# Channel attention and an ELU feed-forward layer on one core: Strassen's h product with another order of block and output products, one seeding copy a unit, high parts rounded by transfers, and other slots for side work

## The chip, the core and the metric

The kernel runs on one core of a Trainium2 chip. The engines named here are TensorE (PE; PEld is its weight load), VectorE (DVE), ScalarE (ACT), GpSimd (POOL) and SyncE (SP, which issues transfers). The metric is the device time of one execution in microseconds (us).

## The reference

q, k and v are fp32 arrays of 4 batches x 6080 tokens x 256 channels. Attention is over channels: q and k are normalised over the tokens, a 256 x 256 matrix per batch goes through a softmax, and v is multiplied with it. The result (24320 x 256) passes through a layer of width 2048 with an ELU and back to 256.

```python
qn = q / (norm(q, axis=1) + 1e-06); kn = k / (norm(k, axis=1) + 1e-06)
s = kn.transpose(0, 2, 1) @ qn / tau
a = softmax(s)                       # max taken off, sum + 1e-09
x = (v @ a).reshape(24320, 256)
h = x @ w_in                         # 256 x 2048
g = where(h > 0, h, exp(min(h, 0)) - 1)
out = g @ w_out                      # 2048 x 256
```

## The kernel before

For each batch the kernel forms W' = a @ w_in once (2048 columns, four quarters `fq` of 512), so that h = v @ W'. The tokens of a batch are 12 chunks `c` of 512 or 496; v comes in, and the output leaves, with channels first. Precision is kept by two-part products: a matrix is rounded to a TensorE format (its high part, `hi`), the rest is its low part (`lo`), and a product is hi·hi + hi·lo + lo·hi, three matmuls that add up in PSUM.

The first batch (to 598 us) is computed in another way and is not touched, apart from the preparation of the next chunk at its end. The other 36 chunks are 144 **units** (c, fq). In a unit the h product is a 2 x 2 block product by Strassen's scheme (Winograd's form) with seven block products of six matmuls each (`product`). Its left operands are blocks and sums of W' (A11, A22, A12, S1 to S4, in `s_tiles`, prepared per batch and quarter), its right operands blocks and sums of v (B11, B21, B22, T1 to T4, per chunk). With U = A11·B11 + S2·T2 the four results are h11 = A11·B11 + A12·B21, h22 = U + S1·T1 + S3·T3, h12 = U + S1·T1 + S4·B22 and h21 = U + S3·T3 + A22·T4. PSUM banks: `bank_a` for h11, two banks `b_0`, `b_1` in turn for U and what is added to it, `bank_e` for S3·T3 and A22·T4. ACT copies `bank_a` into the b bank to seed U, and twice copies the b bank to SBUF (L1468, L1476). VectorE adds `bank_e` to these copies (L1477 for h22, before A22·T4 is added to the bank; L1489 for h21).

Each of the four results goes through the ELU: a ReLU and an exponential on ACT (`relu_exp`, L1175 and L1176), a maximum on VectorE (`largest`, L1179). POOL rounds it (`hi_part`, L1182) and VectorE subtracts (`lo_part`, L1185); the parts stand in `g1` and `g2`, from a ring of three buffers. The output products of a unit (24 matmuls of 512 columns, L1116 to L1118) run in the unit behind it, in groups of one or two items between the block products (`multiply_out`).

Side work fills the engines beside this: v's T sums and block roundings for the next chunk (`t_sum`, `t_hi`, `t_lo`, `b_hi`, `b_lo`), and for the next batch the loads and roundings of q and k (`plan_rows`), the sums of squares, the gram matrix (matmuls put between output matmuls by `beside`), norms and softmax (`plan_soft`) and W' with its S sums (`plan_s`). A planner holds this work as tasks with an engine, a cost in us, a due time and the tasks that they depend on; at fixed places of a unit `spend(engine, budget, now)` writes out the tasks that are due and fit. `now` counts four to a unit (PERIOD). From the first unit on all five engines run in the order in which the code is written, so an instruction that waits holds up all behind it on its engine. Line numbers below are those of the kernel before, unless an order row of the changed kernel is shown.

## Time and profile before

| what | value |
|---|---|
| median of 2 runs | 2263.43 us (2261.64 to 2265.22) |
| profiled execution | 2265.94 us, span 2264.1 us |
| granted TensorE clock | 0.983 |
| busy: PE, PEld | 2156.0 us (95%), 1961.7 us (87%) |
| busy: VectorE, ACT, POOL | 1785.3 us (79%), 1543.3 us (68%), 850.7 us (38%) |
| transfers | 121.23 MB, DMA engines busy 16% by SP's queue |
| first unit's seeding copy | 598.4 us |

A row of the groups gives line, engine, operation, output and inputs, shapes and count, then the busy time and the mean of one in ns, then the idle time just before and what ended it. A row of the waits gives who waited for whom: us in total, times, longest. A row of the order in time gives start, duration, engine, line and, in brackets, idle time and what ended it. PE's busy time counts matmuls that overlap in its pipeline, so that the start of one to the start of the next is the better measure of PE's pace.

### The profile page before, as it was taken

Reading aid. Unit: us, or ns where it says so; the run is one execution under the profiler, and the core shown is the slowest. Engines: PE = TensorE matmul, PEld = TensorE weight load, DVE = VectorE, ACT = ScalarE, POOL = GpSimd, SP = SyncE. Lnnn points to the kernel's source line nnn. Section 1 sums busy time; section 2 is a strip of 40 time slices with the busy share of each in tenths; the row PEclk is TensorE's granted clock in tenths of the full one; section 3 lists DMA queues with packets and bytes.
Section 4 is the critical chain, followed back from the end, with each engine's and each line's share of the span. In section 5 each row is a group of like instructions: output and inputs, shape, how many; then the busy total and the mean of one; then the engine's idle time right before and its main releaser. Section 6 shows DMA issues by size and latency. Waiting matters only on the chain.

```text
span 2264.1 us, 34396 instructions
## 1 busy us (share of the span) xinstructions
PE 2156.0 (95%) x12834; PEld 1961.7 (87%) x12834; DVE 1785.3 (79%) x2514; ACT 1543.3 (68%) x2624; POOL 850.7 (38%) x1063
## 2 busy tenths in 40 slices
PE   9999999999899999899998999998999999999999
PEld 8888888899788888888888888887998888888898
DVE  7997777777788888786788888887778777777776
ACT  6877676667677777666566677775666666666665
POOL 0000000000355555535364555563456443444442
PEclk9999999999999999999999999999999999999999
DMA  9321222211211211100012222110100100100100
...
DMA packets 62567, 121.23 MB, mean 54 GB/s; under 512 B 6208, under 2 KB 16064, under 8 KB 62400
## 3 DMA queue, kind: packets, MB, share of 16 engines
...
q14 instruction: 67, 0.55, 0.1%
q10 hardware_dynamic: 144, 0.13, 0.0%
...
## 4 chain that ended last, share of the span: by engine, by line
PE 55%; DVE 17%; POOL 16%; issue 6%; ACT 5%; DMA 0%; POOLq 0%; ACTq 0%; DVEq 0%
POOL g L1182 7%; PE b L1093 5%; PE po L1116 5%; PE po L1118 5%; PE bank_e L1093 5%; PE po L1117 5%; DVE e_e L1179 4%; PE bank_a L1093 4%; PE ph L428 3%; PE ph L430 3%; PE ph L429 3%; DVE qk L1295 3%; PE po L472 3%; PE po L468 3%; PE po L470 3%
## 5 line engine op out<-in xcount | busy, mean ns | idle before, releaser
L1116 PE MATMUL po<-g,wo 128*128 128x512 f32 (+1 forms) x1158 | 447.6, 387 | 0.8 <-POOL g L1182 0.8
L1118 PE MATMUL po<-g,wo 128*128 128x512 f32 (+1 forms) x1158 | 445.2, 384 | 0.4 <-DVE g L1185 0.4
L1117 PE MATMUL po<-g,wo 128*128 128x512 f32 (+1 forms) x1158 | 445.3, 385 | 0.0
L1182 POOL CAST g<-e_e 128x512 fp32r<-128x512 f32 (+1 forms) x288 | 175.4, 609 | 619.5 <-DVE e_e L1179 605.2
L1093 PE MATMUL bank_e<-t,s 128*128 128x256 f32 (+1 forms) x1728 | 258.4, 287 | 98.7 <-DVE e_u L1477 91.7
L1093 PEld LDWEIGHTS bank_e<-t,s 128*128 128x128 f32 x1728 | 229.9, 198 | 129.2 <-DVE e_u L1477 116.4
L1185 DVE TENSOR_TENSOR g<-held,g 128x512 fp32r<-128x512 f32 (+1 forms) x288 | 283.7, 1021 | 73.3 <-POOL g L1182 73.3
L1182 POOL CAST g<-held 128x512 fp32r<-128x512 f32 (+1 forms) x288 | 228.4, 817 | 202.8 <-DVE held L1179 202.8
L1118 PEld LDWEIGHTS po<-g,wo 128*128 128x128 f32 x1158 | 223.7, 193 | 31.6 <-DVE g L1185 1.0
L1185 DVE TENSOR_TENSOR g<-e_e,g 128x512 fp32r<-128x512 f32 (+1 forms) x288 | 207.3, 720 | 52.7 <-POOL g L1182 42.7
L1093 PEld LDWEIGHTS b<-t,s 128*128 128x128 f32 x1728 | 233.4, 191 | 15.7 <-ACT held L1468 3.2
L1093 PE MATMUL b<-t,s 128*128 128x256 f32 (+1 forms) x1728 | 239.7, 275 | 3.0 <-ACT held L1468 2.1
L1175 ACT ACTIVATE e_e<-e_u 128x512 f32<-128x512 f32 (+1 forms) x144 | 90.3, 627 | 222.0 <-POOL g L1182 163.1
L1117 PEld LDWEIGHTS po<-g,wo 128*128 128x128 f32 x1158 | 225.2, 194 | 15.1
L1116 PEld LDWEIGHTS po<-g,wo 128*128 128x128 f32 x1158 | 224.9, 194 | 13.0 <-POOL g L1182 1.2
L1468 ACT COPY held<-b 128x512 f32<-128x512 f32 (+1 forms) x144 | 83.9, 583 | 169.0 <-PE b L1093 115.8
L1176 ACT ACTIVATE held<-held 128x512 f32<-128x512 f32 (+1 forms) x288 | 180.5, 627 | 9.1
L1176 ACT ACTIVATE e_e<-e_e 128x512 f32<-128x512 f32 (+1 forms) x288 | 180.5, 627 | 9.2
L1093 PE MATMUL bank_a<-s,s 128*128 128x256 f32 (+1 forms) x1296 | 186.2, 281 | 0.0
L1093 PEld LDWEIGHTS bank_a<-s,s 128*128 128x128 f32 x1296 | 178.1, 199 | 7.0
L169 POOL MEMSET raw<- 128x512 f32 x3 | 1.7, 578 | 457.0 <-DVE qk L115 457.0
L115 DVE TENSOR_TENSOR g<-e,g 128x512 fp32r<-128x512 f32 (+1 forms) x192 | 132.2, 688 | 48.9 <-ACT g L114 47.6
...
## 6 DMA issues: line engine op xcount, KB each, us to landing
raw<-in_q_dram SPq DMA_DIRECT2D x76, 256.0 KB, 2.7
raw<-in_k_dram SPq DMA_DIRECT2D x76, 256.0 KB, 3.0
v<-in_v_dram SPq DMA_DIRECT2D x32, 512.0 KB, 3.7
out_dram<-o SPq DMA_DIRECT2D x56, 256.0 KB, 2.0
...
wraw<-w_scr SPq DMA_DIRECT2D x12, 512.0 KB, 3.7
room<-in_q_dram SPq DMA_DIRECT2D x16, 256.0 KB, 5.2
```

Source lines behind the costliest of these rows:

```text
L115: nc.vector.tensor_sub(lo, src, hi.bitcast(F32))
L428: nc.tensor.matmul(ph[:, 0:n], w[:, kt, 0, fs], hi, start=(kt == 0), stop=False)
L1093: nc.tensor.matmul(bank[:, j, 0:hn], w[:, x, js], y, start=(begin and j == 0 and k == 0), stop=(j == 1 and k == 2), skip_group_check=True,)
L1116: yield nc.tensor.matmul(o, wo[:, f, 0, ds], hi, start=begin, stop=False)
L1117: yield nc.tensor.matmul(o, wo[:, f, 1, ds], hi, start=False, stop=False)
L1118: yield nc.tensor.matmul(o, wo[:, f, 0, ds], lo, start=False, stop=end)
L1175: nc.scalar.activation(e, h, AF.Relu, scale=-1.0)
L1176: nc.scalar.activation(e, e, AF.Exp, scale=-1.0)
L1179: nc.vector.scalar_tensor_tensor(e, e, -1.0, h, op0=ALU.add, op1=ALU.max)
L1182: nc.gpsimd.tensor_copy(g[:, :, 0, half, 0:hn], e)
L1185: nc.vector.tensor_sub(g[:, :, 1, half, 0:hn], e, g[:, :, 0, half, 0:hn].bitcast(F32))
L1468: nc.scalar.copy(e["u2"], vb)
```

## The change

- **Order and banks.** The block products keep their order (A11·B11, S3·T3, S2·T2, A12·B21, S1·T1, S4·B22, A22·T4); the output product between the last two now stands behind A22·T4. One bank `bank_b` takes the place of the two b banks. ACT seeds it with one copy of `bank_a` and copies S3·T3 to SBUF (`p7`). VectorE writes `bank_b` + `p7` back into `bank_e` behind S2·T2, and adds `bank_b` to `p7` behind S1·T1 (h22). A22·T4 then completes h21 in `bank_e`, S4·B22 completes h12 in `bank_b`; the ACT copies at L1468 and L1476 and the sum L1489 are gone.
- **High parts by transfers.** Transfers on POOL's queue that change the type take the place of POOL's and ACT's rounding instructions: all four blocks of g (`hi_part`), B11, B21 and B22 (from v in HBM), the w_in parts, the S parts of later batches, and the rows of q and k (read a second time from HBM). The squares of later batches are added to their sums by an accumulating transfer, 1024 elements at once, where VectorE or POOL added 512.
- **Low parts of g.** One subtraction of 1024 elements for g1 and one for g2, in the unit behind (`lo_parts`), where there were four of 512.
- **T.** The sums go from POOL to VectorE (three instructions for four), their rounding from POOL to ACT.
- **Slots.** The queues that several engines shared are gone; a task on POOL or PE may come no sooner than two steps of `now` behind what it needs from another engine, a subtraction behind a transfer no sooner than two steps. Tasks of the first two levels may pass one another. Norm and softmax steps are cut into single instructions, rows come 24 PERIODs to a batch for 23, a batch's plan starts a unit earlier, and budgets and places of `spend` are others.

VectorE in one late unit without side work, before (`e_` and `held` are the ELU blocks, `g1`, `g2` their two parts):

```order
L1179 SCALAR_TENSOR_TENSOR e_e11_5091<-e_e11_5091,bank_a_20589 128x2x248 [waits PE_49,Activation_49]
L1477 TENSOR_TENSOR e_u4_5090<-bank_e_20597,e_u4_5090 128x2x248 [waits Activation_49]
L1185 TENSOR_TENSOR g1_20639<-e_e11_5091,g1_20639 128x2x248 [waits Pool_49]
L1179 SCALAR_TENSOR_TENSOR e_e22_5092<-e_e22_5092,e_u4_5090 128x2x248 [waits DVE_49,Activation_49]
L1489 TENSOR_TENSOR held_5089<-bank_e_20597,held_5089 128x2x248 [waits PE_49]
L1185 TENSOR_TENSOR g2_20674<-e_e22_5092,g2_20674 128x2x248 [waits Pool_49]
```

The same engine at the start of such a unit now (`p7` holds S3·T3, then h22; DMASW are the completions of POOL's transfers):

```order
L1183 SCALAR_TENSOR_TENSOR held_5086<-held_5086,bank_e_20051 128x2x248 [waits PE_49,Activation_49]
L1189 TENSOR_TENSOR g1_20103<-held_5086,g1_20103 128x4x248 [waits DMASW2_49,DMASW0_49,DVE_49]
L1490 TENSOR_TENSOR bank_e_20144<-bank_b_5084,p7_5087 128x2x248 [waits PE_49,Activation_49]
L1189 TENSOR_TENSOR g2_20129<-held_5086,g2_20129 128x4x248 [waits DMASW3_49,DMASW1_49,DVE_49]
L1498 TENSOR_TENSOR p7_5087<-bank_b_5084,p7_5087 128x2x248 [waits DVE_49,PE_49]
```

The subtractions that waited for POOL now wait for transfers, and one stands ahead of each of the two sums. PE from S1·T1 to S4·B22 in a late unit, before (`b_0` is the bank of U, `po_` the output banks):

```order
L1093 MATMUL b_0_5085<-t_1_5094,s_2_4967 128x248 x5
L1116 MATMUL po_47_1_20742<-g1_20740,wo_83 128x496
L1117 MATMUL po_47_1_20742<-g1_20740,wo_83 128x496
L1118 MATMUL po_47_1_20742<-g1_20740,wo_83 128x496
L1116 MATMUL po_47_0_20726<-g1_20740,wo_83 128x496
L1117 MATMUL po_47_0_20726<-g1_20740,wo_83 128x496
L1118 MATMUL po_47_0_20726<-g1_20740,wo_83 128x496
L1093 MATMUL b_0_5085<-s_3_5093,s_2_4967 128x248 [waits Activation_49]
```

PE now, from S2·T2 over A12·B21 to S1·T1:

```order
L1102 MATMUL bank_b_5084<-t_1_5089,s_3_5088 128x248 x5
L1102 MATMUL bank_a_20334<-s_2_4966,s_3_5088 128x248 x6
L1125 MATMUL po_47_0_20189<-g1_20294,wo_83 128x496 [waits DMASW2_49,DMASW0_49]
L1126 MATMUL po_47_0_20189<-g1_20294,wo_83 128x496
L1127 MATMUL po_47_0_20189<-g1_20294,wo_83 128x496 [waits DVE_49]
L1102 MATMUL bank_b_5084<-t_1_5089,s_3_5088 128x248 [waits DVE_49]
```

The next product on the bank waited for ACT and now waits for VectorE, and the output product waits for two transfers and, at its low part, for VectorE. The diff, cut to its core:

```diff
--- before
+++ after
@@ -829,8 +829,12 @@
             lambda: sub(s4, a12, s2),
         )[k]()
 
-    def s_hi(b, fq, lo, hi, copy=nc.scalar.copy):
-        copy(s_tiles[fq][:, lo:hi, 0], x_of(b, fq, 1 + lo, 1 + hi))
+    def s_hi(b, fq, lo, hi, by_dma=False):
+        to, x = s_tiles[fq][:, lo:hi, 0], x_of(b, fq, 1 + lo, 1 + hi)
+        if by_dma:
+            nc.gpsimd.dma_start(to, x)
+        else:
+            nc.scalar.copy(to, x)
...
+    queues = {(e, level): [] for e in (ACT, DVE, POOL, PE, SP) for level in range(4)}
+    GAP = {ACT: 0, DVE: 0, POOL: 2, PE: 2, SP: 0}
 
     class Task:
         def __init__(self, fn, deps, when):
             self.fn, self.deps, self.when, self.done, self.cost = fn, deps, when, None, 0.0
 
-        def ready(self, now, gap):
-            return self.when <= now and all(d.done is not None and d.done + gap <= now for d in self.deps)
-
-    def task(engine, cost, fn, deps=(), when=0, level=1):
+        def ready(self, now):
+            if now < self.when:
+                return False
+            for d in self.deps:
+                if d.done is None:
...
     def spend(engine, budget, now):
-        order = [(engine, 0), (engine, 1), *((x, y) for x in SHARED.get(engine, ()) for y in range(2)), (engine, 2), (engine, 3)]
-        for key in order:
-            queue = queues[key]
-            while queue and queue[0].ready(now, 0):
-                t = queue[0]
-                cost = t.cost if key[0] == engine else t.cost[engine]
-                if cost > budget:
+        for level in range(4):
+            queue = queues[engine, level]
+            while True:
+                able = [t for t in (queue if level < 2 else queue[:1]) if t.ready(now)]
+                if not able or able[0].cost > budget:
                     break
-                queue.pop(0)
-                budget -= cost
-                if key[0] == engine:
-                    t.fn()
-                else:
-                    t.fn({ACT: nc.scalar.copy, DVE: nc.vector, POOL: nc.gpsimd.tensor_copy if key[0] == CAST else nc.gpsimd}[engine])
+                t = able[0]
+                queue.remove(t)
+                budget -= t.cost
+                t.fn()
...
@@ -1009,21 +1020,17 @@
         hn = half_of(c)
         if k == 0:
             state["tt", c] = work.tile([P, 4, HF], F32, tag="raw", bufs=5, name=f"tt_{c}")
-        v = vraw[c]
-        b11, b12 = (v[:, 0, x * hn : (x + 1) * hn] for x in range(2))
-        b21, b22 = (v[:, 1, x * hn : (x + 1) * hn] for x in range(2))
-        t1, t3, t2, t4 = (state["tt", c][:, y, 0:hn] for y in range(4))
-        sub, add = nc.gpsimd.tensor_sub, nc.gpsimd.tensor_add
+        v = vraw[c][:, :, 0 : 2 * hn].rearrange("p k (x t) -> p k x t", x=2)
+        tt = state["tt", c][:, :, 0:hn]
         (
-            lambda: sub(t1, b12, b11),
-            lambda: sub(t3, b22, b12),
-            lambda: add(t2, t3, b11),
-            lambda: sub(t4, b21, t2),
+            lambda: nc.vector.tensor_sub(tt[:, 0:2], v[:, :, 1], v[:, 0]),
+            lambda: nc.vector.tensor_add(tt[:, 2], tt[:, 1], v[:, 0, 0]),
+            lambda: nc.vector.tensor_sub(tt[:, 3], v[:, 1, 0], tt[:, 2]),
         )[k]()
 
     def t_hi(c, k):
         hn = half_of(c)
-        nc.gpsimd.tensor_copy(t_groups[c % 2][:, k : k + 2, 0, 0:hn], state["tt", c][:, k : k + 2, 0:hn])
+        nc.scalar.copy(t_groups[c % 2][:, k : k + 2, 0, 0:hn], state["tt", c][:, k : k + 2, 0:hn])
 
...
@@ -1043,8 +1050,10 @@
         return s_tiles[ring][:, SPARE], vraw[c][:, kt, x * hn : (x + 1) * hn], hn, name
 
     def b_hi(c, k):
-        to, src, hn, _ = block_of(c, k)
-        nc.gpsimd.tensor_copy(to[:, 0, 0:hn], src)
+        to, _, hn, _ = block_of(c, k)
+        _, kt, x = BLOCKS[k]
+        t0 = span(c)[1] + x * hn
+        nc.gpsimd.dma_start(to[:, 0, 0:hn], vT[kt * P : kt * P + P, t0 : t0 + hn])
 
     def b_lo(c, k):
...
@@ -1161,15 +1170,10 @@
         pos[NB - 1, dt] = last_po[dt]
     outs += [None] * 4
 
-    banks_b = [
-        ps.tile([P, 2, HF], F32, tag="w", bufs=WB, name="b_0"),
-        ps.tile([P, 2, HF], F32, tag="o", bufs=8 - KT - WB, name="b_1"),
-    ]
-    for bank in banks_b:
-        nc.tensor.matmul(bank, ones_r, wo[:, 0], start=True, stop=True)
-    held = work.tile([P, 4, 2, HF], F32, tag="qk", bufs=3, name="held")
-    e_tiles = {name: work.tile([P, 2, HF], F32, tag="e", bufs=3, name=f"e_{name}") for name in ("u4", "e11", "e22")}
-    e_tiles |= {name: held[:, x] for x, name in enumerate(("u2", "e12", "e21"))}
+    bank_b = ps.tile([P, 2, HF], F32, tag="o", bufs=8 - KT - WB, name="bank_b")
+    nc.tensor.matmul(bank_b, ones_r, wo[:, 0], start=True, stop=True)
+    held = work.tile([P, 2, 2, 2, HF], F32, tag="qk", bufs=3, name="held")
+    p7 = work.tile([P, 2, HF], F32, tag="e", bufs=3, name="p7")
 
     def relu_exp(e, h):
...
@@ -1179,10 +1183,14 @@
         nc.vector.scalar_tensor_tensor(e, e, -1.0, h, op0=ALU.add, op1=ALU.max)
 
     def hi_part(g, half, e, hn):
-        nc.gpsimd.tensor_copy(g[:, :, 0, half, 0:hn], e)
-
-    def lo_part(g, half, e, hn):
-        nc.vector.tensor_sub(g[:, :, 1, half, 0:hn], e, g[:, :, 0, half, 0:hn].bitcast(F32))
+        nc.gpsimd.dma_start(g[:, 0, :, half, 0:hn], e)
+
+    def lo_parts(g, x, hn):
+        nc.vector.tensor_sub(
+            g[:, 1].rearrange("p j r t -> p (j r) t")[:, :, 0:hn],
+            held[:, x].rearrange("p j r t -> p (j r) t")[:, :, 0:hn],
+            g[:, 0].rearrange("p j r t -> p (j r) t")[:, :, 0:hn].bitcast(F32),
+        )
 
 
...
@@ -1193,16 +1201,14 @@
         if c == NB:
             task(SP, 0, lambda: new_t_group(d), when=t, level=0)
         x = task(SP, 0, lambda: vraw.__setitem__(d, load_v(d)), when=t + PERIOD, level=0)
-        for k in range(4):
-            x = task(POOL, 0.65, lambda k=k: t_sum(d, k), [x], when=t + PERIOD, level=0)
-            if k % 2 == 1:
-                y = task(POOL, 0.65, lambda k=k: t_hi(d, k - 1), [x], when=t + PERIOD, level=0)
-                task(DVE, 0.685, lambda k=k: t_lo(d, k - 1), [y], when=t + PERIOD, level=0)
+        for k in range(3):
+            x = task(DVE, 0.415 if k else 0.685, lambda k=k: t_sum(d, k), [x], when=t + PERIOD, level=0)
+            if k != 1:
+                y = task(ACT, 0.61, lambda k=k: t_hi(d, k), [x], when=t + PERIOD, level=0)
+                task(DVE, 0.685, lambda k=k: t_lo(d, k), [y], when=t + PERIOD, level=0)
         for k, when in enumerate((2 * PERIOD, 3 * PERIOD, 3 * PERIOD + 1)):
-            y = task(POOL, 0.35, lambda k=k: b_hi(d, k), [x], when=t + when, level=0)
-            task(DVE, 0.415, lambda k=k: b_lo(d, k), [y], level=0)
-
-    BOTH = {ACT: 0.61, POOL: 0.65}
+            y = task(POOL, 0.55, lambda k=k: b_hi(d, k), when=t + when, level=0)
+            task(DVE, 0.415, lambda k=k: b_lo(d, k), [y, x], level=0, late=2)
 
     def plan_s(b, fq, t, norm_deps, early=False):
...
@@ -1447,64 +1468,71 @@
             plan_chunk(c)
         spend(SP, 1, now)
         assert (b, fq) in s_ready, (b, fq, u)
-        e = {name: t[:, :, 0:hn] for name, t in e_tiles.items()}
+        e11, e12, e21, e22 = (held[:, x, :, half, 0:hn] for x, half in ((0, 0), (0, 1), (1, 0), (1, 1)))
+        vp = p7[:, :, 0:hn]
         bank_a = ps.tile([P, 2, HF], F32, tag="w", bufs=WB, name="bank_a")
+        bank_e = ps.tile([P, 2, HF], F32, tag="w", bufs=WB, name="bank_e")
+        va, vb, ve = (bank[:, :, 0:hn] for bank in (bank_a, bank_b, bank_e))
+
         product(bank_a, c, fq, "A11", "B11", True)
-        bank_b = banks_b[u % 2]
-        va, vb = bank_a[:, :, 0:hn], bank_b[:, :, 0:hn]
+        if before is not None:
+            before[0]()
         nc.scalar.copy(vb, va)
-        bank_e = ps.tile([P, 2, HF], F32, tag="w", bufs=WB, name="bank_e")
-        ve = bank_e[:, :, 0:hn]
         product(bank_e, c, fq, "S3", "T3", True)
+        nc.scalar.copy(vp, ve)
         multiply_out(2, now)
+        spend(POOL, 3.9, now)
+        spend(ACT, 2.2, now)
+        spend(DVE, 2.8, now)
         if before is not None:
-            before()
-        spend(ACT, 1.9, now)
-        spend(POOL, 4.3, now)
-        spend(DVE, 2.5, now)
+            before[1]()
         product(bank_b, c, fq, "S2", "T2")
+        nc.vector.tensor_add(ve, vb, vp)
+        if before is not None:
+            before[2]()
         product(bank_a, c, fq, "A12", "B21")
+        relu_exp(e11, va)
+        spend(POOL, 0.6, now + 1)
         multiply_out(1, now)
-        nc.scalar.copy(e["u2"], vb)
         product(bank_b, c, fq, "S1", "T1")
-        relu_exp(e["e11"], va)
-        largest(e["e11"], va)
+        nc.vector.tensor_add(vp, vb, vp)
+        largest(e11, va)
         g1 = work.tile([P, 2, 2, 2, HF], F32R, tag="g", bufs=3, name="g1")
-        hi_part(g1, 0, e["e11"], hn)
-        spend(POOL, 1.3, now + 2)
-        multiply_out(2, now)
-        nc.scalar.copy(e["u4"], vb)
-        nc.vector.tensor_add(e["u4"], ve, e["u4"])
+        hi_part(g1, 0, e11, hn)
+        multiply_out(2, now + 2)
+        spend(ACT, 1.1, now + 2)
+        spend(DVE, 1.4, now + 2)
         product(bank_b, c, fq, "S4", "B22")
-        spend(ACT, 1.25, now + 2)
-        lo_part(g1, 0, e["e11"], hn)
-        spend(DVE, 1.0, now + 2)
-        multiply_out(1, now)
         product(bank_e, c, fq, "A22", "T4")
-        relu_exp(e["e22"], e["u4"])
-        largest(e["e22"], e["u4"])
-        multiply_out(2, now)
+        relu_exp(e22, vp)
+        largest(e22, vp)
+        multiply_out(1, now + 2)
         g2 = work.tile([P, 2, 2, 2, HF], F32R, tag="g", bufs=3, name="g2")
-        hi_part(g2, 1, e["e22"], hn)
-        nc.vector.tensor_add(e["u2"], ve, e["u2"])
-        relu_exp(e["e12"], vb)
-        relu_exp(e["e21"], e["u2"])
-        lo_part(g2, 1, e["e22"], hn)
-        largest(e["e12"], vb)
-        hi_part(g1, 1, e["e12"], hn)
-
-        def before(e=e, g1=g1, g2=g2, hn=hn):
-            largest(e["e21"], e["u2"])
-            hi_part(g2, 0, e["e21"], hn)
-            lo_part(g1, 1, e["e12"], hn)
-            lo_part(g2, 0, e["e21"], hn)
+        hi_part(g2, 1, e22, hn)
+        spend(DVE, 0.7, now + 2)
+        relu_exp(e12, vb)
+        relu_exp(e21, ve)
+        largest(e12, vb)
+        hi_part(g1, 1, e12, hn)
+        multiply_out(2, now + 2)
+
+        def finish(e21=e21, ve=ve, g2=g2, hn=hn):
+            largest(e21, ve)
+            hi_part(g2, 0, e21, hn)
+
+        before = (
+            finish,
+            lambda g1=g1, hn=hn: lo_parts(g1, 0, hn),
+            lambda g2=g2, hn=hn: lo_parts(g2, 1, hn),
+        )
```

155 lines of the change are left out of this document (88 added, 67 removed).

## The prediction

> **What bounds the kernel now.** I read the first part of the page, then the waits, then the once-a-unit copy by its line, then the order in time around one long unit. First the page and the copy that opens each unit (L1455, `bank_b` from `bank_a`).
>
> ```profile
> PE 2156.0 (95%) x12834; PEld 1961.7 (87%) x12834; DVE 1785.3 (79%) x2514; ACT 1543.3 (68%) x2624; POOL 850.7 (38%) x1063
> ...
> L1455 ACT COPY b<-bank_a x144: 557/578/590, 598.4 to 2243.4; 128x512 f32<-128x512 f32 x96, 128x496 f32<-128x496 f32 x48
> ...
> 1993.84 0.58 ACT L1455 COPY b<-bank_a 128x512 f32<-128x512 f32 x1
> 2003.71 0.58 ACT L1455 COPY b<-bank_a 128x512 f32<-128x512 f32 x1
> 2013.59 0.58 ACT L1455 COPY b<-bank_a 128x512 f32<-128x512 f32 x1
> 2027.15 0.57 ACT L1455 COPY b<-bank_a 128x512 f32<-128x512 f32 x1 [0.24 <-PE bank_a L1093]
> ...
> 2163.41 0.57 ACT L1455 COPY b<-bank_a 128x496 f32<-128x496 f32 x1
> 2173.13 0.56 ACT L1455 COPY b<-bank_a 128x496 f32<-128x496 f32 x1
> ...
> 633.99 0.58 ACT L1455 COPY b<-bank_a 128x512 f32<-128x512 f32 x1
> 645.15 0.58 ACT L1455 COPY b<-bank_a 128x512 f32<-128x512 f32 x1
> ```
>
> There are 144 units, from 598.4 to the end at 2264.1: 1665.7 us. An undisturbed unit takes 9.87 us with 512 tokens (2003.71 less 1993.84) and 9.72 with 496; one that also multiplies a group of rows into the gram matrix takes 11.16 (645.15 less 633.99). The unit that begins at 2013.59 takes 13.56 with the same matmuls as its neighbour. This is why:
>
> ```profile
> PEld bank_e L1093 <- DVE e_u L1477: 116.4, 63, 4.0
> DVE g L1185 <- POOL g L1182: 116.0, 331, 1.9
> ...
> PE bank_e L1093 <- DVE e_u L1477: 91.7, 48, 3.6
> ...
> DVE t L1031 <- POOL t L1026: 90.1, 70, 1.3
> ...
> 2018.42 1.21 DVE L1031 TENSOR_TENSOR t<-tt,t 128x512 fp32r<-128x512 f32 x1 [1.30 <-POOL t L1026]
> 2020.92 0.69 DVE L1031 TENSOR_TENSOR t<-tt,t 128x512 fp32r<-128x512 f32 x1 [1.29 <-POOL t L1026]
> 2021.53 0.68 DVE L1179 SCALAR_TENSOR_TENSOR e_e<-e_e,bank_a 128x512 f32<-128x512 f32 x1
> 2022.13 0.69 DVE L1477 TENSOR_TENSOR e_u<-bank_e,e_u 128x512 f32<-128x512 f32 x1
> ...
> 2020.10 0.38 PE L1117 MATMUL po<-g,wo 128*128 128x512 f32 x1
> 2020.32 0.38 PE L1118 MATMUL po<-g,wo 128*128 128x512 f32 x1
> 2022.87 0.94 PE L1093 MATMUL bank_e<-t,s 128*128 128x256 f32 x6 [2.18 <-DVE e_u L1477]
> ...
> 2024.35 0.63 PE L1116 MATMUL po<-g,wo 128*128 128x512 f32 x1
> 2024.77 0.63 PE L1117 MATMUL po<-g,wo 128*128 128x512 f32 x1
> ```
>
> VectorE stands twice behind POOL's rounding of the next chunk's T matrices, so L1477 is late; it must read `bank_e` before PE may add A22·T4 to it, and PE waits 2.18 us. After the wait, matmuls start 0.42 us apart (2024.77 less 2024.35) where they take 0.217 undisturbed (20.32 after 20.10), so a long wait is paid nearly twice. The floor of the unit stage is what PE needs without waits: 96×9.87 + 48×9.72 + 48 gram units (24 groups of rows in each of two batches) ×(11.16−9.87) + 96 matmuls for W' (two batches, four quarters, two halves, six each) ×0.217 = 948+467+62+21 = 1497. The profiled run (2265.94, span 2264.1, 1.8 around it; median of the shown runs 2263.43, 2.5 lower) loses 169 us to waits. With none it would be 598.4+1497+1.8 = **2097**.
>
> **The change part by part.** *The sums.* S3·T3 is copied to SBUF (`p7`); VectorE writes U+S3·T3 into `bank_e` right after S2·T2, three block products ahead of A22·T4, which then finds its bank ready. L1477's wait goes as a place: 92 us as PE shows it, up to the whole 169 with the slow restarts. What is late next is VectorE's two sums, each read by the next product on the single `bank_b`. As the rows of the section on the change show, `bank_b` was released for the next product by ACT and is now by VectorE, and the output product ahead of S1·T1 waits for two transfers and for VectorE. So VectorE's queue decides, and there each of the two sums (L1490, L1498) stands behind a low-part subtraction (L1189) that waits for transfers of the unit before. Queued behind that wait on VectorE are the sum, the maxima and all side work; PE waits for the sum with its next product, and ACT for the second sum with e22. That closes a loop, once round per unit: sum into `bank_e`, low parts of g2, sum into `p7`, ReLU and exp of e22, ReLU and exp of e12, its maximum, the transfer of its high part (L from the maximum's end to landing), low parts of g1, and again the sum. Prices:
>
> ```profile
> L1489 DVE TENSOR_TENSOR held<-bank_e,held 128x512 f32<-128x512 f32 (+1 forms) x144 | 97.7, 679 | 1.5 <-PE bank_e L1093 1.4
> ...
> L182 DVE TENSOR_TENSOR acc<-acc,sq x38: 1214/1225/1226, 10.5 to 502.0; 128x1024 f32<-128x1024 f32 x38
> ...
> L1175 ACT ACTIVATE held<-held 128x512 f32<-128x512 f32 (+1 forms) x144 | 90.5, 628 | 50.8 <-DVE held L1489 47.5 <-POOL g L1182 3.4
> ...
> L1175 ACT ACTIVATE held<-b 128x512 f32<-128x512 f32 (+1 forms) x144 | 83.0, 576 | 0.2 <-PE b L1093 0.2
> ...
> L1176 ACT ACTIVATE held<-held 128x512 f32<-128x512 f32 (+1 forms) x288 | 180.5, 627 | 9.1
> ...
> L1179 DVE SCALAR_TENSOR_TENSOR held<-held,b 128x512 f32<-128x512 f32 (+1 forms) x144 | 97.3, 676 | 0.0
> ...
> raw<-in_q_dram SPq DMA_DIRECT2D x76, 256.0 KB, 2.7
> raw<-in_k_dram SPq DMA_DIRECT2D x76, 256.0 KB, 3.0
> v<-in_v_dram SPq DMA_DIRECT2D x32, 512.0 KB, 3.7
> out_dram<-o SPq DMA_DIRECT2D x56, 256.0 KB, 2.0
> ...
> room<-in_q_dram SPq DMA_DIRECT2D x16, 256.0 KB, 5.2
> ```
>
> 0.68 + 1.22 + 0.68 + 0.63 + 0.63 + 0.58 + 0.63 + 0.68 + 1.22 = 6.95, with some 0.15 for handovers (my estimate) 7.1 + L. No transfer from SBUF to SBUF, none that rounds and none from POOL's queue is in this trace, so L is bounded by others of 256 KB: 2.0 (the store) below, 3.7 (twice the bytes) above, 5.2 where many are queued. I take 3.0, the second of two loads issued together, since it lands in SBUF as this one does and e22's transfer goes out just ahead of e12's. The loop is then 10.1, and the 96 units without gram, whose PE needs 9.81 on average (9.87 and 9.72), lose 0.29 each: 28 us. At L = 2.0 they lose nothing, at 3.7 they lose 96×0.99 = 95. Gram units (11.16) have 1.06 to spare, so for them the loop is hidden by PE up to L = 4.06.
>
> The Trainium skill (DMA: Bandwidth & Descriptors, "Anatomy of one DMA — SWDGE (gpsimd) path") gives such transfers 2.0 us plus the bytes at 436 GB/s, 2.6 us here: by it the loop would be 9.7 and the 28 us none.
>
> *Casts leave POOL and ACT.* The 576 roundings of g leave POOL, and with them the time that they and VectorE's subtractions took from each other: the same subtraction of 512 elements takes 0.72 us in one place and 1.02 in the other, and the same rounding 0.61 and 0.82.
>
> ```profile
> L1182 POOL CAST g<-held 128x512 fp32r<-128x512 f32 (+1 forms) x288 | 228.4, 817 | 202.8 <-DVE held L1179 202.8
> ...
> L1182 POOL CAST g<-e_e 128x512 fp32r<-128x512 f32 (+1 forms) x288 | 175.4, 609 | 619.5 <-DVE e_e L1179 605.2 <-PE bank_e L1093 9.4 <-PE bank_a L1093 2.5
> ...
> L1185 DVE TENSOR_TENSOR g<-held,g 128x512 fp32r<-128x512 f32 (+1 forms) x288 | 283.7, 1021 | 73.3 <-POOL g L1182 73.3
> ...
> L1185 DVE TENSOR_TENSOR g<-e_e,g 128x512 fp32r<-128x512 f32 (+1 forms) x288 | 207.3, 720 | 52.7 <-POOL g L1182 42.7
> ...
> L1278 POOL TENSOR_TENSOR acc<-acc,sq 128x512 f32<-128x512 f32 x71 | 113.7, 1619 | 0.1
> ...
> 2060.22 0.41 SPq L397 DMA_DIRECT2D v<-in_v_dram  x1
> ```
>
> VectorE's four subtractions, 2×1.02+2×0.72 = 3.48 us a unit, become two of 1.22: 1.0 us less, off the loop but cover for its side work. ACT, 68% busy, loses a copy (0.58) in each unit. POOL gains 848 transfers: 4.75 in a unit without gram (four of g, and three blocks of B in every four units), 7.75 with (two loads of rounded rows and one accumulation more). At 0.4 (SP's issue) to 1.62 (POOL's longest instruction) each, that is 1.9 to 7.7 of 9.81 us, and 3.1 to 12.6 of 11.16. I take the low end, for the issue is work of the same sort as SP's, and price it at nothing; the high end is the third rival. SP's own queue keeps its loads and stores.
>
> *Side work.* T sums go to VectorE ahead of g1's low parts: 0.68+2×0.42 = 1.5 us, beneath the transfer's cover there (L less the 1.3 of e21's ELU), 1.7: nothing; uncovered, 36×1.5 = 54. T's low parts stand ahead of e22's maximum while ACT still works on e22 for 1.26 us, 0.68 of it taken by e11's maximum: 72×0.1 = 7 not covered. Norm, softmax and S stages fill the first slot's budget of 2.8 against that 1.7 in some 16 units (a batch's norm and softmax cost about 9 us by the code's own costs, so four units, twice; and eight S sets): 16×1.1 = 18, between 0 and 16×2.8 = 45. Gram units move some 1 MB more from POOL's queue beside the loop; if that makes L longer by the 2.2 us between 3.0 and 5.2, 1.06 of it is spare and 48×1.1 = 55 is lost, otherwise 0; I take 10.
>
> Sum on the profiled run: 2097+28+7+18+10 = 2160; on the median 2158. Predicted **2160**.
>
> **Rivals.** *The wait comes back as a wait for the landing* (L about 3.8, or transfers whose descriptors wait for a VectorE instruction, 0.68 to 1.22): 96×(7.1+3.8−9.81) = 105, and with the 35 of side work 2097+105+35 = 2237, no change. For it: `DVE g<-POOL g` shows VectorE waiting 331 times already for a rounding of 0.61 to 0.82 us. Against: the 2.0 row. The Trainium skill (SBUF — State Buffer, "Who interferes with whom") says descriptor writing is locked out by VectorE's two-port modes, and that tensor_tensor has none; by it this would not happen here. 0.16.
>
> *It does not do what it says:* T's rounding now makes VectorE wait for ACT as it did for POOL; one wait of 2.2 us in each of the 36 chunks stays, though at another product: 36×2.2 = 79, 2097+79+28+35 = 2239. Against: ACT is 68% busy and the subtraction is placed a slot later. 0.06.
>
> *Slower: POOL's queue.* If one transfer holds it 1.62 us, 1.2 more than SP's issue, and e12's stands behind what is left of e22's, 0.6, L is 3.0+1.2+0.6 = 4.8: 96×2.09 = 200, gram units 48×1.4 = 67, 2097+267+35 = 2399. It is slower than before by 2% from L about 4.4 (96×1.7+48×0.35 = 180 on top of 2132). For it: the POOL rows here run from 0.61 to 1.62 us, none as short as SP's issue. Against: nothing shows its issue. 0.21.
>
> **How the numbers follow.** Forecast 0.57, the others 0.16, 0.06, 0.21. Two per cent (2218, 2309) is about what a measurement of this kernel can tell from no change: faster 0.57, same 0.22, slower 0.21. The range starts at the floor, 2100, and ends at L = 4.6 (2340), inside the slow case; some 0.15 lies outside.
>
> **What would show it.** The copy that opens a unit should come every 9.9 to 10.2 us in the late units, with no 13 us units; `bank_e` waiting for VectorE gone; PE's remaining waits on `bank_b` for L1490 and L1498; VectorE idle before L1189 for a transfer; L near 3.0; L1189 at 1.22. Wrong if L is over 4, or POOL is busy over 80%.

## The result, and the profile after

The changed kernel takes **2333.3 us** (median of two runs, 2332.99 to 2333.62), against 2263.43 before: a ratio of 1.031 (95% interval 1.026 to 1.035). It is slower by 3 per cent, where 2160 was forecast. The profiled execution took 2332.99, its span is 2331.2. In the late units, which multiply no rows, the forecast holds in sum; most of the time is lost in the stages that do.

The copy that opens a unit is L1480 now. Its rows in the order in time of the changed kernel, at units 4, 28, 100 and 143, counted from 0 (start, us, engine, line), then the same four of the kernel before without the first, which the prediction shows:

```profile
647.49 0.57 ACT L1480 COPY bank_b<-bank_a 128x512 f32<-128x512 f32 x1
...
976.85 0.57 ACT L1480 COPY bank_b<-bank_a 128x512 f32<-128x512 f32 x1
...
1872.61 0.57 ACT L1480 COPY bank_b<-bank_a 128x512 f32<-128x512 f32 x1 [0.88 <-PE bank_a L1102]
...
2308.08 0.56 ACT L1480 COPY bank_b<-bank_a 128x496 f32<-128x496 f32 x1 [0.87 <-PE bank_a L1102]
```

```profile
939.70 0.58 ACT L1455 COPY b<-bank_a 128x512 f32<-128x512 f32 x1
...
1789.01 0.58 ACT L1455 COPY b<-bank_a 128x512 f32<-128x512 f32 x1
...
2243.43 0.57 ACT L1455 COPY b<-bank_a 128x496 f32<-128x496 f32 x1
```

The 43 units from 100 to 143 took 454.4 us and take 435.5, 19 less. The 24 units from 4 to 28, most of them gram units, took 294.6 and take 329.4, 35 more; units 52 to 76, the second batch's, took 294.4 and take 316.1. Rows are now multiplied up to units 32 and 81, where they ended in units 27 and 75, and the units 28 to 48 and 76 to 96 together take 21 us more.

The page of the changed kernel (busy time of the engines; VectorE's low parts of g; then transfers with their count, size and median us from issue to landing), and behind it its waits (engine, tile and line, what it waited for: us in total, times, longest):

```profile
PE 2200.9 (94%) x12833; PEld 1967.5 (84%) x12833; DVE 1599.7 (69%) x2322; ACT 1419.1 (61%) x2380; POOL 633.4 (27%) x909
...
L1189 DVE TENSOR_TENSOR g<-held,g 128x1024 fp32r<-128x1024 f32 (+1 forms) x288 | 351.4, 1220 | 242.4 <-DMA g<-held 216.2
...
g<-held POOLq DMA_DIRECT2D x384, 256.0 KB, 2.5
...
acc<-sq POOLq DMA_DIRECT2D x46, 512.0 KB, 6.6
...
qk<-in_q_dram POOLq DMA_DIRECT2D x46, 256.0 KB, 6.6
```

```profile
DVE g L1189 <- DMA g<-held: 216.2, 112, 6.2
ACT sq L1287 <- DMA acc<-sq: 212.2, 29, 10.1
...
PE po L1125 <- DMA g<-held: 69.9, 33, 4.6
...
DVE t L1038 <- ACT t L1033: 59.8, 35, 2.3
...
PE bank_e L1102 <- DVE held L1183: 3.7, 10, 0.8
```

PE's 91.7 us of waiting for VectorE on `bank_e` are down to 3.7. In their place stand two waits for landings. VectorE waits 216 us for g, and ACT waits 212 us, in 29 places, for the accumulating transfer (L1290) to release the one buffer `sq` for the next group's square (L1287). The accumulate's median landing is 6.6 us after its issue, its 512 KB being twice the bytes of a transfer of g, which lands after 2.5.

One gram unit of the changed kernel in order of time, 15.25 us long. It is the first unit of its chunk; most such gram units take 15 to 17 us, most of the others 11 to 13:

```profile
1474.29 0.68 DVE L1183 SCALAR_TENSOR_TENSOR held<-held,bank_b 128x512 f32<-128x512 f32 x1
1474.33 0.72 POOL L1186 DMA_DIRECT2D g<-held  x1 [1.11 <-issue]
1474.43 0.38 SPq L397 DMA_DIRECT2D v<-in_v_dram  x1
...
1475.05 0.57 ACT L1480 COPY bank_b<-bank_a 128x512 f32<-128x512 f32 x1
1475.27 1.45 POOL L1186 DMA_DIRECT2D g<-held  x2 [0.21 <-issue]
...
1476.72 0.95 POOL L1290 DMA_DIRECT2D acc<-sq  x1
1477.30 0.92 POOL L1306 DMA_DIRECT2D qk<-in_q_dram  x1
...
1481.00 1.23 DVE L1189 TENSOR_TENSOR g<-held,g 128x1024 fp32r<-128x1024 f32 x1 [4.96 <-DMA g<-held]
...
1484.67 1.06 ACT L1287 ACTIVATE sq<-raw 128x1024 f32<-128x1024 f32 x1 [8.54 <-DMA acc<-sq]
1485.63 0.58 ACT L1179 ACTIVATE held<-bank_a 128x512 f32<-128x512 f32 x1
...
1490.30 0.57 ACT L1480 COPY bank_b<-bank_a 128x512 f32<-128x512 f32 x1
```

The transfer of e12's high part goes out at 1475.27 and has landed by 1481.00, after 5.7 us. Two transfers were issued within the microsecond ahead of it, e22's (1474.33) and SP's load of the next chunk's v (1474.43, 512 KB); e21's, the accumulate and the rows' transfers go out right behind it. So the delay of this one transfer can't be put down to those behind it alone. From the end of e12's maximum (1474.97) to the landing, the prediction's L is 6.0. The square has been ACT's next instruction since 1476.1 and stands there 8.54 us, until the accumulate issued at 1476.72 has landed. The unit's ReLU of e11 (1485.63) is queued behind it, though PE had completed its bank at 1477.65. These are two separate delays in one unit, and the experiments are there to price them apart.

How busy the DMA engines were in such stretches is read from the view of windows (window, its length, busy time of PE, PEld, DVE, ACT and POOL with counts, granted clock, the DMA engines' busy share, GB/s), for this gram unit, a calm one, units 4 to 28, and units 100 to 143:

```profile
1475.30:1481.00 5.70, 2.35 (x18) 2.10 (x17) 0.74 (x2) 0.83 (x2) 3.42 (x5) 1.00 1.12 290
...
2003.70:2006.30 2.60, 2.60 (x20) 2.44 (x19) 2.14 (x4) 1.56 (x4) 1.43 (x3) 1.00 0.85 224
...
647.50:976.80 329.30, 288.88 (x1729) 256.20 (x1728) 192.95 (x276) 169.31 (x282) 114.73 (x168) 0.94 0.75 190
1872.60:2308.10 435.50, 430.93 (x2841) 395.25 (x2839) 303.95 (x425) 276.43 (x473) 139.12 (x202) 1.00 0.52 136
```

```profile
645.15:939.70 294.55, 274.62 (x1763) 250.11 (x1762) 253.80 (x325) 207.94 (x364) 164.27 (x185) 0.99 0.18 58
```

The last row is units 4 to 28 of the kernel before: its DMA engines were busy 0.18 of the time, where they are 0.75 now. In the gram unit above they had hardly any free time while e12's transfer was under way (the share adds up the records of the packets, which can overlap, so it can pass 1). The same rows show a part of the loss that lies behind the waits: over units 4 to 28 the granted clock is 0.94, where it was 0.99, and PE is busy 289 us with 1729 matmuls, where the last kernel below needs 264 for 1730 at 1.00. So some 25 us of these units are matmuls that took longer, as the prediction had seen them do behind a wait.

### The profile page after: what moved, and what is told of

Read it like the earlier page. It is cut to its first block, busy times and chain, and to the rows that moved or that the text cites. A ratio compares the mean times of both kernels' runs of the same rounds, so it can differ in the third digit from the quotient of the medians.

```text
span 2331.2 us, 35484 instructions
## 1 busy us (share of the span) xinstructions
PE 2200.9 (94%) x12833; PEld 1967.5 (84%) x12833; DVE 1599.7 (69%) x2322; ACT 1419.1 (61%) x2380; POOL 633.4 (27%) x909
## 5 line engine op out<-in xcount | busy, mean ns | idle before, releaser
L1186 POOL DMA_DIRECT2D g<-held x576 | 409.8, 712 | 1061.1 <-issue 390.0
L1189 DVE TENSOR_TENSOR g<-held,g 128x1024 fp32r<-128x1024 f32 (+1 forms) x288 | 351.4, 1220 | 242.4 <-DMA g<-held 216.2
L1180 ACT ACTIVATE held<-held 128x512 f32<-128x512 f32 (+1 forms) x576 | 360.6, 626 | 18.3
L1102 PEld LDWEIGHTS bank_b<-t,s 128*128 128x128 f32 x1728 | 238.6, 201 | 48.2 <-DVE bank_e L1490 33.6
L1102 PE MATMUL bank_b<-t,s 128*128 128x256 f32 (+1 forms) x1728 | 263.4, 291 | 11.1 <-ACT bank_b L1480 3.2
L1179 ACT ACTIVATE held<-bank_a 128x512 f32<-128x512 f32 (+1 forms) x144 | 84.8, 589 | 241.9 <-PE bank_a L1102 103.2
L1287 ACT ACTIVATE sq<-raw 128x1024 f32<-128x1024 f32 x46 | 48.8, 1060 | 218.0 <-DMA acc<-sq 212.2
L114 ACT CAST g<-e 128x512 fp32r<-128x512 f32 (+1 forms) x192 | 116.7, 608 | 69.6 <-DVE e L445 37.6
L1183 DVE SCALAR_TENSOR_TENSOR held<-held,bank_a 128x512 f32<-128x512 f32 (+1 forms) x144 | 97.1, 674 | 85.7 <-ACT held L1180 85.7
L1480 ACT COPY bank_b<-bank_a 128x512 f32<-128x512 f32 (+1 forms) x144 | 81.6, 566 | 111.4 <-PE bank_a L1102 89.2
L1179 ACT ACTIVATE held<-p 128x512 f32<-128x512 f32 (+1 forms) x144 | 89.7, 623 | 91.3 <-DVE p L1498 91.3
```

What stands on the lines that cost most here:

```text
L114: nc.scalar.copy(hi, src)
L1102: nc.tensor.matmul(bank[:, j, 0:hn], w[:, x, js], y, start=(begin and j == 0 and k == 0), stop=(j == 1 and k == 2), skip_group_check=True,)
L1179: nc.scalar.activation(e, h, AF.Relu, scale=-1.0)
L1180: nc.scalar.activation(e, e, AF.Exp, scale=-1.0)
L1183: nc.vector.scalar_tensor_tensor(e, e, -1.0, h, op0=ALU.add, op1=ALU.max)
L1186: nc.gpsimd.dma_start(g[:, 0, :, half, 0:hn], e)
```

## The experiments

Two theories stood against each other. **A**: the square that waits for the accumulate stands in ACT's queue in front of the unit's ReLU and exp. **B**: the extra bytes (accumulate and rows, 1 MB a group of rows) delay the transfers of g that VectorE waits for. Edits are cut to their core, and line numbers shift by a few in the edited kernels. Each run was timed beside the kernel before, and the ratio to that (95% interval) stands in brackets.

### Each part undone by itself

The squares added on VectorE:

```
-    nc.gpsimd.dma_start(acc, sq, accum_op=ALU.add)      # task on POOL, level 2
+    nc.vector.tensor_add(acc[:, y], acc[:, y], sq[:, y]) # two tasks on VectorE, level 0
```

> The sums of the squares go back from the accumulating transfer (512 KB, landed after 6.6 us) to two additions of 512 elements on VectorE (0.69 us each); all else as in the changed kernel (2333). Theory A, the next square stands in ACT's queue ahead of the unit's ReLU and exp until the accumulate has landed in front of its one buffer (212 us of ACT's idle time): that wait goes, long gram units fall from 18.5 to about 13, time 2180 to 2230. Theory B, g's transfers land late because some 1 MB more per group passes through POOL's transfer queue: half the extra bytes go, so about half of the 173 us above the forecast, time 2240 to 2280, and VectorE's wait for g (216 us) falls to about half.

Measured: 2257.9 (0.997, 0.996 to 0.999). 75 us come back, not the 100 to 150 of theory A; the time, and VectorE's wait for g at half of 216, are what theory B had forecast. The waits of this kernel show another reason, a new wait, which a later run tests:

```profile
DVE g L1189 <- DMA g<-held: 106.5, 74, 4.0
...
DVE acc L1291 <- ACT sq L1287: 84.8, 29, 6.0
```

My additions may be placed in the slot in which the square itself was placed. VectorE reaches them before ACT reaches the square, and stands there 85 us. The wait had moved from ACT's queue to VectorE's.

The rows rounded on ACT:

```
-    nc.gpsimd.dma_start(hl[:, 0, y], rows_of[:, 2 * g : 2 * g + n, :])   # for q and k
+    nc.scalar.copy(hl[:, 0], raw)                        # low parts without late=2
```

> The rounded rows of q and k come again from a copy on ACT (1.05 us a group) instead of two 256 KB transfers from POOL's queue; the accumulating transfer stays. Theory A: ACT still stands 8 to 10 us before a square, so the time stays at 2310 to 2350, and ACT's wait for the accumulate stays near 200 us, unless the accumulate itself lands sooner with less beside it. Theory B: half the extra bytes and two of the three extra transfers go, VectorE's wait for g falls to about half, time 2240 to 2280.

Measured: 2303.2 (1.016, 1.009 to 1.023), between the two: VectorE's wait for g fell to 85 us, as in theory B, and ACT's wait for the accumulate to 139, with fewer bytes beside it. But VectorE now stands 74 us (45 times) for ACT's rounding ahead of the rows' low parts, which this edit lets stand in the slot of that rounding.

The square later, by the planner's rule alone:

```
-    s = task(ACT, 1.05, square, [x, *acc_done], when=t + 2, level=3)
+    s = task(ACT, 1.05, square, [x, *acc_done], when=t + 2, level=3, late=2)
```

> Only the planner's rule for one task changes: a square may be placed at the earliest half a unit (5 us) after the accumulate of the square before it was placed, where now it may follow in the same slot. All transfers stay. Theory A: the square finds its buffer free or nearly so (the accumulate lands after 6.6 us), ACT's wait of 212 us falls below 60, time 2200 to 2250. Theory B: the transfers are the same and so is the time, 2320 to 2340.

Measured: 2281.2 (1.007, 1.005 to 1.009), between the two; ACT's wait falls to 54 us, and VectorE waits 195 us for g as it did (216). So neither theory alone: A is real, and the larger part of the loss is left.

Squares on VectorE and rows on ACT:

> Squares added on VectorE and rows rounded on ACT, so that of the transfers which the change put on POOL's queue in a gram unit only g's four and the T blocks' stay. Under both theories the gram units then run close to what their PE work needs: time 2130 to 2200. Should it stay above 2250, neither the accumulate nor the rows' transfers are the cause, and the casting transfers of g themselves or the new order of the block products lose the time in gram units.

Measured: 2314.8 (1.021, 1.018 to 1.025), above the bound that I had set, and far above the sum of the two parts. By my own words this would blame g's transfers or the new order. It doesn't show that: the additions stand 80 us behind the square on VectorE here too, and the rows' low parts (here 14 us behind ACT) stand in the place that the last run shows to be costly. The same kernel with both placed later was not run, so what it would say of g's transfers stays open.

### The place of the transfers, and of the additions

The rows' transfers and the accumulate in a slot of their own, behind e11's transfer:

```
     hi_part(g1, 0, e11, hn)
+    spend(ROWS, 3.9, now + 2)      # a queue of the planner for these tasks alone
```

> The rows' two transfers and the accumulate leave the slot at the unit's start, where they go out just behind e21's transfer, and go out behind e11's instead, whose landing is needed half a unit later; everything else as in the changed kernel (2333). Theory B (the extra bytes delay the g transfer that they follow): VectorE's wait for g falls from 216 us to about 100 and the time by 50 to 90, to 2245 to 2285. Theory A alone (the square behind the accumulate): the square may now follow the accumulate in the very next slot of ACT, ahead of e22's ReLU, so the wait stays at some 200 us and the time at 2310 to 2350.

Measured: 2508.9 (1.109, 1.106 to 1.112). VectorE's wait for g falls to 133 us, towards theory B's 100, and the time rises by 175 us; both theories are wrong on the time. What else happens stands in its waits:

```profile
DVE held L1183 <- ACT held L1180: 419.5, 301, 10.6
ACT sq L1287 <- DMA acc<-sq: 333.2, 44, 10.9
...
PE bank_b L1102 <- ACT bank_b L1480: 165.4, 37, 6.7
DVE g L1189 <- DMA g<-held: 132.9, 97, 4.9
```

The square now follows the accumulate into the next slot in 44 of 46 groups, in front of e22's ReLU and of the next unit's copy, and PE waits for that copy.

The same with the late square:

> The same move of the transfers, and the square placed at the earliest half a unit after the accumulate before it. The run with the second edit alone gave 2281, with VectorE still waiting 195 us for g. If place decides, that wait falls below 100 and the time is 2190 to 2240, below the kernel before. If the number of bytes on POOL's queue decides wherever they stand, time 2270 to 2290.

Measured: 2375.0 (1.050, 1.047 to 1.053), outside both readings. ACT's wait is all but gone (30 us), and VectorE's for g is 151, not below 100; but the rows' low parts now stand on VectorE 87 us for the rows' landing (37 times, up to 5.4), and in front of g's low parts. Away from one queue's waits, the transfers met another's.

Rows on ACT and the square late:

> Rows rounded on ACT (2303 alone) and the square late (2281 alone): only the accumulate's 512 KB remain of the extra transfers. If the two losses are separate their gains add, 30 + 52: 2250. If ACT's part has become the bound in gram units (three operations of 1.06 us where two were), it stays at 2280 to 2300.

Measured: 2294.0 (1.014, 1.010 to 1.018): the gains don't add, as the second reading says, though not for its reason: VectorE stands 83 us (45 times, up to 7.1) for ACT's rounding ahead of the rows' low parts, and the last run shows, in the kernel with POOL's casts, that this place, and not ACT's time, is what costs.

Squares on VectorE, half a unit late:

```
-    task(DVE, 0.685, lambda: add(y), [s], level=0)
+    task(DVE, 0.685, lambda: add(y), [s], level=0, late=2)
```

> Squares added on VectorE as in the run that gave 2258, but each addition placed at the earliest half a unit after its square; in that run VectorE stood 85 us (29 times, up to 6.0) in its queue for a square that ACT had not reached. If that was what kept it from the forecast, the wait falls below 20 and the time to 2190 to 2225. If the rows' transfers beside g's are the rest, the wait for g stays near 106 us and the time at 2235 to 2260.

Measured: **2210.7** (0.977, 0.973 to 0.980), faster than the kernel before. The wait of 85 us is gone from the list, and the edit of one number was worth 47 us. All of g's and the rows' transfers are still there, and VectorE still waits 137 us for g. Units 4 to 28 of this kernel:

```profile
645.02:915.97 270.95, 267.77 (x1746) 244.24 (x1745) 214.97 (x317) 173.03 (x283) 99.31 (x153) 1.00 0.72 197
```

The DMA engines are as busy there (0.72) as in the changed kernel (0.75), yet the units take 271 us where those took 329. So the busy share by itself does not make the loss.

### Buffer, bytes, or the adding itself

A second buffer for the squares:

```
+    other_sq = [work.tile([P, 2, C], F32, tag="e", bufs=3) for y in range(2)]   # even groups
```

> The changed kernel with a second buffer for the squares (every second group's square in two pieces of 512 elements, with two accumulating transfers of 256 KB); order and bytes as they were. Theory A, the one buffer: ACT's wait of 212 us goes to nothing and the time to about 2215, as with the additions on VectorE. Theory B, the bytes beside g's transfers: the wait goes too, but VectorE's wait for g stays near 200 us, and the time is that of the late square, 2265 to 2290.

Measured: 2266.7 (1.002, 1.000 to 1.003): 67 us come back, ACT's wait for the accumulate is gone, VectorE's wait for g stays at 202. It is theory B's figure: A is worth 67 us here, and 56 more lie between this and the additions on VectorE.

A plain transfer in place of the accumulating one, in the kernel with the late square:

> The kernel with the late square (2281), its accumulating transfer replaced by a plain one of the same 512 KB between the same tiles: the sum of the squares is left out (each group overwrites the one before). If it is the bytes beside g's transfers that cost what is left above 2211, the time stays at 2265 to 2290 and the transfer lands after some 5 us; if it is that it adds (reads its target first), it lands after some 3 us and the time is 2215 to 2235.

Measured: 2235.5 (0.988, 0.985 to 0.991), from 2281.2; this kernel leaves out the sum of the squares. The rows for the landing are, with the accumulate (late square), and plain:

```profile
acc<-sq POOLq DMA_DIRECT2D x46, 512.0 KB, 5.7
```

```profile
acc<-sq POOLq DMA_DIRECT2D x46, 512.0 KB, 3.9
```

The same bytes between the same tiles land 1.8 us sooner when they are not added, and 46 of the 70 us between 2281 and 2211 are gone. So the adding is what costs, more than the 512 KB, and it costs by its longer landing: ACT's wait for this transfer falls from 54 us to 11 and VectorE's for the rows, whose transfers stand behind it, from 29 to 5, while VectorE's wait for g stays (195 and 197).

Squares added on POOL:

> The squares added on POOL (two additions of 512 elements, 1.2 to 1.6 us each) instead of on VectorE, in POOL's slot at the unit's start, where POOL stands idle for some 8 us between e21's transfer and e11's. If VectorE's queue is what is left in gram units, its 1.4 us a group less gives 2190 to 2210. If POOL's additions hold back a transfer of g, or slow VectorE's instructions beside them, 2225 to 2260.

Measured: 2266.7 (1.003, 1.001 to 1.004), beyond even the worse reading. Its waits, and the page's row of the low parts:

```profile
ACT sq L1287 <- POOL acc L1291: 77.4, 30, 5.1
```

```profile
L1189 DVE TENSOR_TENSOR g<-held,g 128x1024 fp32r<-128x1024 f32 (+1 forms) x288 | 380.6, 1322 | 211.7 <-DMA g<-held 189.7 <-issue 21.8
```

ACT's square now waits for POOL's additions behind the one buffer, VectorE's low parts of g take 1.32 us, where they took 1.22, and VectorE waits 190 us for g.

The high parts of g rounded by POOL's cast, in the kernel with the late additions:

```
-    nc.gpsimd.dma_start(g[:, 0, :, half, 0:hn], e)
+    nc.gpsimd.tensor_copy(g[:, 0, :, half, 0:hn], e)
```

> The kernel with late additions on VectorE (2211), with the high parts of g rounded again by POOL's cast (0.61 to 0.82 us) instead of casting transfers (2.5 us to landing); the order of the block products stays new. If the landing is what is left in the loop, it gets shorter by some 1.7 us at each of two places and the time falls to 2180 to 2200. If POOL's casts and VectorE's subtractions take from each other as in the kernel before (a subtraction of 512 elements 0.72 or 1.02 us), the low parts get longer by 0.6 to 0.8 each and the time is 2205 to 2240.

Measured: 2178.5 (0.963, 0.960 to 0.966), a little better than the first reading. The row of the low parts in the kernel with the late additions, and in this one:

```profile
L1189 DVE TENSOR_TENSOR g<-held,g 128x1024 fp32r<-128x1024 f32 (+1 forms) x288 | 352.4, 1224 | 146.8 <-DMA g<-held 136.8 <-issue 6.5 <-DVE bank_e L1491 1.9
```

```profile
L1189 DVE TENSOR_TENSOR g<-held,g 128x1024 fp32r<-128x1024 f32 (+1 forms) x288 | 358.0, 1243 | 0.5 <-POOL g L1186 0.5
```

VectorE's idle time ahead of them goes from 147 us to 0.5, while POOL's casts beside them make them no slower than 1.24 us. Casting transfers for g do not pay in this kernel.

### Untangling

Only that edit, on the changed kernel itself, so that the accumulate and the rows' transfers have their queue without g:

> The changed kernel (2333) with one edit: the high parts of g rounded by POOL's cast instead of casting transfers. The accumulate and the rows' transfers stay, and no transfer of g shares their queue. If the square behind the accumulate costs what the second buffer gave back (66 us), wherever g goes, and the rest of the loss was the bytes beside g's transfers, the time is 2178 + 66, 2230 to 2260. If the accumulate is harmless without g's transfers (it lands sooner), 2180 to 2205.

Measured: 2251.9 (0.996, 0.994 to 0.997). This is the first reading. The wait of ACT and the window of units 4 to 28 in this kernel:

```profile
ACT sq L1287 <- DMA acc<-sq: 199.7, 30, 8.6
```

```profile
646.30:944.60 298.30, 274.95 (x1729) 245.51 (x1729) 199.84 (x277) 168.38 (x282) 119.12 (x168) 0.99 0.51 125
```

The accumulate lands hardly sooner (6.0 for 6.6), with the DMA engines busy 0.51 of these units, and ACT waits nearly as long (200 us for 212). This is the accumulate without g's transfers, 2252 less 2176 (the run below), 76 us; most of it will be theory A, but the rows' transfers land later beside it too (6.3 us for 3.0, and VectorE waits 24 us for them).

The rows on ACT in the kernel with POOL's casts, and that kernel again:

> The kernel that gave 2178 (additions on VectorE, POOL's casts for g), with the rows rounded on ACT: beside the order of the block products, only T's rounding on ACT and the transfers for the T blocks, S and the input weights are left of the change. If the rows' transfers pay (they take 1.05 us a group off ACT, whose square stands beside them), the time rises by 13 to 57 as it did in the two pairs before, to 2190 to 2235. If they paid only where g's transfers were in the way, 2170 to 2185.

> The kernel that gave 2178, timed against the kernel before in three rounds: 2177 to 2180, 3.6 to 3.8 per cent faster.

Measured: 2238.9 (0.990, 0.988 to 0.991), and 2175.8 (0.962, 0.960 to 0.963). The first is a little above its upper range. Taken by themselves these say that the rows' transfers are worth 63 us. The last run tests whether it is the transfers or the place of VectorE's subtraction, which in my edit may stand in the slot of ACT's copy:

```
-    los = [task(DVE, 0.685, lo, [h, x], level=2, late=0) for y in range(2)]
+    los = [task(DVE, 0.685, lo, [h, x], level=2, late=2) for y in range(2)]
```

> The kernel with the rows on ACT (2239), in which each low part of the rows may stand on VectorE in the very slot in which ACT's copy was placed, with one edit: it is placed at the earliest half a unit later. If the rows' transfers paid only because their low parts were placed late already, the time falls to 2175 to 2195, that of the kernel with the rows' transfers. If ACT's 1.05 us a group more are the price, it stays at 2225 to 2240, and VectorE still waits for ACT's ReLU and exp in gram units.

Measured: **2169.2** (0.958, 0.956 to 0.961), the fastest of all. The 63 us were the place, not the transfers. Units 4, 28, 100 and 143 of this kernel, and the window between the first two:

```profile
645.20 0.57 ACT L1476 COPY bank_b<-bank_a 128x512 f32<-128x512 f32 x1 [1.14 <-PE bank_a L1102]
...
909.71 0.57 ACT L1476 COPY bank_b<-bank_a 128x512 f32<-128x512 f32 x1 [0.82 <-PE bank_a L1102]
...
1719.74 0.57 ACT L1476 COPY bank_b<-bank_a 128x512 f32<-128x512 f32 x1 [0.82 <-PE bank_a L1102]
...
2148.45 0.56 ACT L1476 COPY bank_b<-bank_a 128x496 f32<-128x496 f32 x1 [0.81 <-PE bank_a L1102]
```

```profile
645.20:909.70 264.50, 263.74 (x1730) 242.55 (x1729) 228.46 (x312) 190.28 (x300) 81.50 (x115) 1.00 0.23 70
```

The 24 units take 264.5 us, with PE busy 263.7 of them; before the change they took 294.6, after it 329.4. This kernel has the new order of the block products, the sums, the seeding copy and T's rounding on ACT, and of the transfers only those for the blocks of v (B11, B21, B22), S and the input weights.

Where the 164 us between the changed kernel and this one lie, as the runs have them:

| step | time, us | gain |
|---|---|---|
| the changed kernel | 2333.3 | |
| second buffer for the squares | 2266.7 | 67 |
| squares added on VectorE, late, instead | 2210.7 | 56 more |
| g's high parts by POOL's casts | 2175.8 | 35 more |
| rows on ACT, low parts late | 2169.2 | 7 more |

The last 7 us are 0.3 per cent and close to the scatter of these runs. The parts are not independent. Without the accumulate g's transfers cost 35 us (2211 less 2176), and with it 81 (2333 less 2252); without g's transfers the accumulate costs 76, and with them 123.

## Why the prediction was wrong

**The floor and the wait on `bank_e`: right.** The wait went (91.7 to 3.7 us), and with the extra transfers taken away the same order of block products runs at 2169, where I forecast 2160 for the change and 2097 without any wait. What the change gains is in that kernel, but its parts were not taken apart: T's rounding, which made the 13 us units, left POOL as well. Whether the planner's new rules (late tasks) would have helped the order before, too, was not tried. The floor itself is some 11 us low: from the last unit's opening copy (2243.43) to the end of the span (2264.1) the kernel before takes 20.7 us, where the floor counts one unit of 9.72.

**The loop in calm units: right in L, a little high in sum.** Here is the late unit between 2004.68 and 2014.56 in the changed kernel's order of time:

```profile
2002.70 0.69 DVE L1183 SCALAR_TENSOR_TENSOR held<-held,bank_b 128x512 f32<-128x512 f32 x1 [0.52 <-PE po L1127]
2002.99 1.42 POOL L1186 DMA_DIRECT2D g<-held  x2 [1.01 <-PE po L1127]
...
2004.68 0.57 ACT L1480 COPY bank_b<-bank_a 128x512 f32<-128x512 f32 x1 [0.88 <-PE bank_a L1102]
...
2006.34 1.23 DVE L1189 TENSOR_TENSOR g<-held,g 128x1024 fp32r<-128x1024 f32 x1 [0.28 <-DMA g<-held]
...
2014.56 0.57 ACT L1480 COPY bank_b<-bank_a 128x512 f32<-128x512 f32 x1 [0.87 <-PE bank_a L1102]
...
2016.36 0.69 DVE L1038 TENSOR_TENSOR t<-tt,t 128x512 fp32r<-128x512 f32 x1 [1.96 <-ACT t L1033]
...
2025.08 0.57 ACT L1480 COPY bank_b<-bank_a 128x512 f32<-128x512 f32 x1 [0.88 <-PE bank_a L1102]
```

L is 2006.34 less 2003.39: 2.95, where 3.0 was taken. The transfer itself, the second of two from 2002.99 on, landed 2.5 us after its issue. The Trainium skill (DMA: Bandwidth & Descriptors, "Anatomy of one DMA — SWDGE (gpsimd) path") gives 2.6 for its bytes, an estimate by its fit, and here the trace agrees. The unit takes 9.88 us, not 10.1, so the 28 us of that term did not come: successive instructions overlap by some 0.05 to 0.1 us, where I had added 0.15 for handovers. The first rival's L of 3.8 in every such unit did not come either.

**T's sums and low parts.** The sums were hidden as priced. Of the low parts, which I had at 7 us, one set stands ahead of g1's low parts and waits 1.96 us for ACT's rounding (2016.36; 59.8 us in 35 waits); that unit takes 10.52 for 9.87, 36×0.65 = 23. It is the second rival's mechanism at a third of its price. So the late units come out at the forecast (435.5 us for 43, 434 at 10.1 each), though the loop's 0.29 each of it, 12 us, did not come: T's low parts, 0.65 in every fourth unit, and smaller delays stand in their place. That the sum fits is luck.

**POOL's issue: right in its price.** It holds POOL 0.71 us a transfer of g, where 0.4 was taken, and POOL is busy 27%, so nothing as a price was near enough. The third rival's mechanism did not come, though its sign did: it had put the longer L into every unit and on POOL, and the longer L came nearly all in gram units, from the transfers themselves. Its sum is wrong, too: at L = 4.8 a gram unit loses 7.1 + 4.8 less 11.16, 0.74 us and not 1.4, so its case is 2368 by its own terms, not 2399.

**The step that failed** is the one sentence on gram units: "Gram units move some 1 MB more from POOL's queue beside the loop", taken at 10 us, between 0 and 55. It failed twice. The size of L was bounded by 5.2; in the 62 units that multiply rows now its median is 3.4, but it passes 5.2 in 15 of them and reaches 7.2 (6.0 in the unit shown, 2.9 in the median late unit). I had measured queueing by loads at the program's start and not asked what else would be under way. And the main cost was no matter of L: the accumulate's landing became the release of the one buffer `sq`, in front of which ACT's in-order queue stands. I had counted its issue on POOL and its bytes, but not who waits for its end. Before, that was an addition that had been done in time; the planner counts a transfer as done when it is placed, so it puts the next square right behind it. The two together are worth 157 us (2333 less 2176), 117 of them in units 4 to 28 and 52 to 76, and with them left out the forecast is 16 us low. That nearness is no proof of the sum: the kernel of 2176 has no landing of g in its loop at all, so its 43 late units take 429 us and not the forecast's 434, while other stages, the end that the floor leaves out among them, take more. My own sign for a wrong forecast, L above 4, is what the trace shows, in gram units.

**Norm, softmax and S stages** (18 us) were not taken apart. The 40 units from 28 to 48 and 76 to 96, in which most of them lie, took 481 us, 77 more than 40 loops of 10.1, and 454 in the fastest kernel. The floor has 21 of this for W', and rows are now multiplied in eleven of these units; how much of the rest is this term's stays open.
